# First pair's scores through ScalarE and GpSimd, loads of 112 rows instead of 128, half of the first f on ScalarE's queue

## The chip, the cores and the metric

The kernel runs on one core of a Trainium2 chip. The time is that of the device for one execution, in microseconds (us); the runs shown are three executions, given by their median. A profile is one more execution, recorded instruction by instruction; all its times count from the start of its span.

The engines, as the profile names them: PE (TensorE) multiplies matrices into PSUM, and PEld is its loading of weights; DVE (VectorE), ACT (ScalarE) and POOL (GpSimd) do elementwise work and scans; SP (SyncE) here only issues DMAs. SPq, DVEq and ACTq are the sequencers of those engines.

## The reference

```python
f = 1.0 / (1.0 + np.exp(-f_logit))                 # B, H, S, D = 4, 8, 768, 48
for t in range(S):
    state = f[:, :, t, :, None] * state + einsum('bhd,bhde', k[:, :, t], v[:, :, t])
    y[:, :, t] = einsum('bhd,bhde->bhe', q[:, :, t], state)
x = y as (3072 tokens, 384)
logits = x @ phi                                   # 32 slots, 4 for each of 8 experts
slot_input = softmax(logits over tokens).T @ x
slot_out[e] = relu(slot_input[e] @ w1[e]) @ w2[e]  # 384 -> 1024 -> 384
out = softmax(logits over slots) @ slot_out
```

It is a gated linear attention whose output goes through a mixture of experts with soft routing. All is float32.

## The kernel before

**Tiles.** The 32 heads are worked on as 16 pairs. In a tile of a pair the channels are rows: the first head has rows 0 to 47, the second rows 64 to 111 (`PW = 112`), and tokens are columns (768). The arrays in memory have 128 rows for each pair, so rows 48 to 63 and 112 to 127 are filler. A sequence is cut into 6 chunks of 128 tokens.

**One pair.** With the short names that the plan uses, and the lines of the profile:

- `lf`, `lk`, `lq`, `lv`: loads of f, k, q, v (L325, L754), issued by SP.
- `e` (ACT, L330) is exp(-f) with a running sum, `ln` (ACT, L334) is ln(1 + that), `L` (DVE, L338) its cumulative sum within each chunk, a scan.
- `g` and `p` (ACT, L341 and L344) are exp(L) and exp(-L). `dk` (L347) multiplies k by g, `dq` (L347) multiplies q by p; these run on POOL or DVE by pair.
- `pbx` and `pend` (POOL, L321 and L359) copy the decays at the ends of chunks, from p, for the state.
- `kt` (PE, L367) transposes k, `kte` (L321, tile kta) copies that out of PSUM.
- `sc` (PE, L379) are the scores k·q of each chunk for both heads, in two halves of three chunks each. `mask` (DVE, L384) multiplies them by a triangle of ones and zeros on the way from PSUM to the tile scb: two instructions for each pair.
- `kv` (PE, L413), then `scan` (DVE, L417) makes the states. `ia` (PE, L404) multiplies the masked scores by v, `ie` (PE, L427) adds q times state, `ye` (ACT, L321, tile yT) copies the result out of PSUM.
- `lg`, `xtr`, `xe` make the logits and the transposed y for the experts.

For pair 0 everything up to `dq` is done in two halves of 384 tokens, so that it starts on half a load.

**What sets the order.** Each operation is declared with an engine, an assumed duration and a due time; the class `Plan` runs a model of the engines over them, and the instructions are then written out in the order that the model found. Every engine works through its own instructions strictly in that order, whatever happens on the chip. For the first three pairs the table `START` sets due times by hand. SP's loads have due times too, with an assumed rate, and no more than eight loads are outstanding: the ninth waits until the first has landed, and so on. The score tile is double (scb), the PSUM is cut into three units of two banks (`a`) and two of one bank (`b`), which the plan hands out; `sc`, `kt`, `y` and `xt` share the three.

Two things at the start of the program touch the change: ACT's first instruction loads its table of functions (L229), and the first two loads of SP are the halves of pair 0's f (L754).

After the 16 pairs the experts follow (PE lines L502 to L712), whose weights w1 and w2 SP loads all along, into tiles that have come free.

Of the kernel before, what the change touches and what calls it, by code (L numbers as in the profile page):

```python
# [11 lines left out]
ALU = mybir.AluOpType  # L12
# [201 lines left out]
def gla_soft_moe_kernel(ctx: ExitStack, tc: tile.TileContext, q, k, f, v, vt, phi, w1, w2, out):  # L214
# [14 lines left out]
    nc.scalar.preload_act_table_set("natural_log_exp_and_others")  # L229
# [11 lines left out]
    fb = [P([128, S], f"fb{i}") for i in range(N_F)]  # L241
    Lb = [P([128, S], f"Lb{i}") for i in range(N_L)]
# [83 lines left out]


# [44 lines left out]
    def score(o, i, h):  # L372

        u = unit(("sc", i, h))
        for m in range(3):
            cs = slice(C * (3 * h + m), C * (3 * h + m) + C)
            for r in range(2):
                rs = slice(64 * r, 64 * r + D)
                nc.tensor.matmul(  # L379
                    u[:, 512 * r + C * m : 512 * r + C * m + C], kb[i % N_K][rs, cs], qb[i % N_Q][rs, cs], start=True, stop=True,  # L380
                )

# [344 lines left out]
    def warm(due, n, us=0.9):  # L727
# [11 lines left out]
        L=(-99, -98), dk=(-97, -95), dq=(-96, -94.5), mask=(-94.3, -92),  # L739
        kt=(-99, -96), sc=(-98, -95),  # L740
    )
    for n, (name, i) in enumerate(

        [("e", 1), ("ln", 1), ("kte", 0), ("e", 2), ("g", 1), ("p", 1), ("ln", 2), ("e", 3), ("ye", 0), ("kte", 1), ("g", 2), ("p", 2), ("ln", 3), ("ye", 1)]
# [3 lines left out]
        + [("pbx", 0), ("dk", 1), ("pend", 0)]  # L748
# [3 lines left out]

    def load_half(o, dst, src, cs):
        nc.sync.dma_start(dst[:, cs], src[:, cs])  # L754

    def attention(i):
# [12 lines left out]
        if i == 0:  # L769
            for h, cs in enumerate(HALVES):  # L770
                op("lf", {"SP": 0.45}, load_half, fb[0], f[0], cs, w=F_[h : h + 1], due=-99, kb=192)
        else:
            op("lf", {"SP": 0.45}, load, fb[i % N_F], f[i], w=F_, due=z - (25 if i > 1 else 18.5), kb=384)
        op("lk", {"SP": 0.45}, load, kb[i % N_K], k[i], w=K, due=z - 14, kb=384)
        if i == 0:

            for h, cs in enumerate(HALVES):
                op("lq", {"SP": 0.45}, load_half, qb[0], q[0], cs, w=Q[h : h + 1], due=-12 + 0.7 * h, kb=192)
        else:
            op("lq", {"SP": 0.45}, load, qb[i % N_Q], q[i], w=Q, due=z - 12, kb=384)  # L780
# [222 lines left out]
    for o in order:  # L1003
# [4 lines left out]
        new = list(nc.cur_bb.bb.instructions)[n0:]  # L1008
        if o.name in ("lw1", "lw2"):
# [20 lines left out]
    def general_pair(i):  # L1030
# [4 lines left out]
        nc.sync.dma_start(ft, f[i].unsqueeze(1).broadcast_to([128, NE4, S]))  # L1035
        nc.sync.dma_start(kq, k[i])
        nc.sync.dma_start(qt, q[i])
# [47 lines left out]
def _layout(inputs):  # L1085
# [52 lines left out]
```

## Time and profile before

| what | value |
|---|---|
| median of 3 runs | 168.49 us (167.91 to 168.71) |
| profiled execution, its own time | 168.29 us |
| its span, first to last instruction | 166.6 us |
| mean granted clock of TensorE | 0.984 |
| busy share of the span: PE, DVE, ACT, POOL | 92%, 70%, 57%, 54% |
| moved by DMA | 54.05 MB, mean 325 GB/s |
| the three loads of f, k and q of a pair | 384 KB each |

A row of the timeline reads: start, duration (both in us), engine, line, operation, written tile <- read tiles, shape, count; in brackets the idle time of the engine just before, and what ended it. Durations overlap a little: the next instruction of an engine starts up to 0.1 us before the recorded end of the one before. A busy PE is not PE at its peak. A row of the list of groups gives busy time in total and the mean of one instruction in ns. In the chain of waits each piece is followed back from the last instruction to what released it.

### The profile page before, as it was taken

Reading aid. Unit: us, or ns where it says so; the run is one execution under the profiler, and the core shown is the slowest. Engines: PE = TensorE matmul, PEld = TensorE weight load, DVE = VectorE, ACT = ScalarE, POOL = GpSimd, SP = SyncE. Lnnn points to the kernel's source line nnn. Section 1 sums busy time; section 2 is a strip of 40 time slices with the busy share of each in tenths; the row PEclk is TensorE's granted clock in tenths of the full one; section 3 lists DMA queues with packets and bytes.
Section 4 is the critical chain, followed back from the end, with each engine's and each line's share of the span. In section 5 each row is a group of like instructions: output and inputs, shape, how many; then the busy total and the mean of one; then the engine's idle time right before and its main releaser. Section 6 shows DMA issues by size and latency. Waiting matters only on the chain.

```text
span 166.6 us, 6386 instructions
## 1 busy us (share of the span) xinstructions
PE 153.7 (92%) x2724; PEld 123.3 (74%) x2724; DVE 116.6 (70%) x167; ACT 94.2 (57%) x166; POOL 89.9 (54%) x87
## 2 busy tenths in 40 slices
PE   5999999999999999999998999999899999999800
PEld 2367879889998969889896889988655449788700
DVE  4899999989979876898996989838432216043330
ACT  5899597967977949678783872631521121232310
POOL 5108969889889886897997889660000001000000
PEclk9999999999999999999999999999999999999985
DMA  5999999999999999999997559999999792055784
GB/s 134 320 407 370 390 399 398 399 398 393 395 393 397 397 397 399 396 398 398 398 377 248 182 173 293 340 363 407 398 398 389 233 360 85 6 215 211 281 295 151
DMA packets 20609, 54.05 MB, mean 325 GB/s; under 512 B 2288, under 2 KB 2912, under 8 KB 20576
## 3 DMA queue, kind: packets, MB, share of 16 engines
q1 hardware_dynamic: 20432, 53.34, 86.2%
q8 instruction: 22, 0.36, 0.9%
q10 hardware_dynamic: 144, 0.26, 0.4%
q14 instruction: 11, 0.09, 0.1%
HBM read 48.87 MB, written 4.72 MB: 322 GB/s over the span
## 4 chain that ended last, share of the span: by engine, by line
PE 67%; DVE 14%; POOL 5%; issue 4%; DMA 3%; ACT 3%; SPq 1%; POOLq 0%; ACTq 0%; DVEq 0%
PE sc L379 10%; PE y L404 9%; PE po L670 7%; PE up L625 7%; PE y L427 6%; PE kv L413 5%; PE kt L367 5%; DVE Lb L338 5%; PE xt L438 4%; PE pl L459 3%; PE pf L712 3%; DMA kb<-in_k_dram 3%; DVE scb L384 3%; POOL ce L545 2%; PE pi L502 2%
## 5 line engine op out<-in xcount | busy, mean ns | idle before, releaser
L347 POOL TENSOR_TENSOR kb<-kb,gb 112x768 f32<-112x768 f32 x15 | 27.4, 1830 | 16.3 <-ACT gb L341 12.8
L338 DVE TENSOR_TENSOR_SCAN Lb<-starts,fb 112x768 f32<-112x768 f32 (+1 forms) x17 | 35.1, 2063 | 1.6 <-ACT fb L334 1.6
L384 DVE TENSOR_TENSOR scb<-sc,mask 128x768 f32<-128x768 f32 x32 | 29.2, 950 | 4.0 <-PE sc L379 3.9
L321 POOL COPY pbx<-pb 112x240 f32<-112x240 f32 x16 | 26.6, 1663 | 4.6 <-ACT pb L344 4.6
L379 PE MATMUL sc<-qb,kb 48*128 48x128 f32 x384 | 26.5, 282 | 0.5 <-DVE kta L321 0.4
L404 PE MATMUL y<-scb,va 128*48 128x128 f32 (+1 forms) x384 | 25.9, 276 | 0.0
L379 PEld LDWEIGHTS sc<-qb,kb 48*128 48x128 f32 x384 | 22.9, 187 | 3.4 <-DVE kta L321 0.6
L321 ACT COPY yT<-y 112x768 f32<-112x768 f32 x16 | 12.8, 798 | 19.6 <-PE y L427 19.6
L347 POOL TENSOR_TENSOR qb<-qb,pb 112x768 f32<-112x768 f32 x13 | 23.7, 1827 | 0.0
L404 PEld LDWEIGHTS y<-scb,va 128*48 128x48 f32 (+1 forms) x384 | 21.9, 130 | 0.8 <-DVE scb L384 0.4
L545 POOL TENSOR_TENSOR ce<-ce,cm 128x256 f32<-128x256 f32 x4 | 4.6, 1156 | 29.7 <-DVE cm L542 29.3
L321 DVE COPY kta<-kt 128x672 f32<-128x672 f32 x14 | 11.8, 846 | 7.6 <-PE kt L367 7.6
L341 ACT ACTIVATE gb<-Lb 112x768 f32<-112x768 f32 (+1 forms) x17 | 13.7, 805 | 4.9 <-DVE Lb L338 4.9
L334 ACT ACTIVATE fb<-fb,one 112x768 f32<-112x768 f32 (+1 forms) x17 | 15.2, 897 | 0.6
L330 ACT ACTIVATE fb<-fb 112x768 f32<-112x768 f32 (+1 forms) x17 | 13.7, 805 | 2.7 <-DMA fb<-in_f_dram 2.7
L427 PE MATMUL y<-qb,sb 48*48 48x128 f32 x320 | 14.6, 285 | 0.0
L413 PE MATMUL kv<-va,kta 128*64 128x48 f32 (+1 forms) x384 | 14.4, 220 | 0.0
L413 PEld LDWEIGHTS kv<-va,kta 128*64 128x64 f32 (+1 forms) x384 | 12.4, 130 | 2.6 <-ACT kta L321 0.8
L344 ACT ACTIVATE pb<-Lb 112x768 f32<-112x768 f32 (+1 forms) x17 | 13.5, 792 | 0.0
L427 PEld LDWEIGHTS y<-qb,sb 48*48 48x48 f32 x320 | 11.1, 162 | 2.7 <-DVE sb L417 2.4
L367 PE MATMUL kt<-ident,kb 112*128 112x112 f32 x96 | 12.7, 266 | 0.2 <-POOL kb L347 0.2
L321 DVE COPY w1a<-pf 128x512 f32<-128x512 f32 x9 | 5.8, 687 | 9.5 <-ACT w1a L321 9.5
(154 smaller groups left out, 276.9 us busy)
## 6 DMA issues: line engine op xcount, KB each, us to landing
w1a<-in_w_dram SPq DMA_DIRECT2D x34, 384.0 KB, 7.6
kb<-in_k_dram SPq DMA_DIRECT2D x16, 384.0 KB, 7.4
fb<-in_f_dram SPq DMA_DIRECT2D x15, 384.0 KB, 7.3
qb<-in_q_dram SPq DMA_DIRECT2D x15, 384.0 KB, 7.3
va<-in_v_dram SPq DMA_DIRECT2D x16, 288.0 KB, 7.3
out_dram<-w1a SPq DMA_DIRECT2D x6, 512.0 KB, 3.5
scb<-in_w_dram SPq DMA_DIRECT2D x4, 384.0 KB, 6.9
out_dram<-w1a SPq DMA_DIRECT2D x5, 256.0 KB, 3.9
```

The costliest lines, as they stand in the source:

```text
L321: {"ACT": nc.scalar.copy, "DVE": nc.vector.tensor_copy, "POOL": nc.gpsimd.tensor_copy}[o.eng](dst, src)
L330: nc.scalar.activation(t, t, AF.Exp, scale=-1.0, accum_out=esum[:, n : n + 1])
L334: nc.scalar.activation(t, t, AF.Ln, bias=one[:PW])
L338: nc.vector.tensor_tensor_scan(Lb[i % N_L][:PW, cs], flat(starts)[:PW, cs], fb[i % N_F][:PW, cs], 0.0, op0=ALU.mult, op1=ALU.add)
L341: nc.scalar.activation(gb[i % N_G][:PW, cs], Lb[i % N_L][:PW, cs], AF.Exp)
L347: (nc.vector if o.eng == "DVE" else nc.gpsimd).tensor_tensor(t, t, by, op=ALU.mult)
L367: nc.tensor.transpose(u[:, C * m : C * m + PW], kb[i % N_K][:PW, C * m : C * m + C], ident[:PW, :PW])
L379: nc.tensor.matmul(u[:, 512 * r + C * m : 512 * r + C * m + C], kb[i % N_K][rs, cs], qb[i % N_Q][rs, cs], start=True, stop=True,)
L384: nc.vector.tensor_tensor(scb[i % N_SC][:, :, h], un["sc", i, h].rearrange("p (r x) -> p r x", r=2)[:, :, : 3 * C].rearrange("p r (m t) -> ...
L404: nc.tensor.matmul(u[rows(at), y_cols(m)], va[:, v0 : v0 + (D if at else 64)], scb[i % N_SC][:, r, h, m % 3], start=m % 3 == 0, stop=False ...
L413: nc.tensor.matmul(u[rows(r), :, m], ktb[i % N_KT][:, m, rows(r)], vb[i % N_V][:, m, r], start=True, stop=True)
L427: nc.tensor.matmul(u[at : at + D, y_cols(m)], sb[i % N_S][rs, :, m - 1], qb[i % N_Q][rs, C * m : C * m + C], start=False, stop=m in (2, 5) ...
```

## The change

Four edits, all about the start of the program, except that the second holds for all pairs.

1. Half 0 of pair 0's scores is no longer multiplied by the triangle on DVE. ACT copies it from PSUM (`smc`), and POOL then clears the upper triangle in place with one affine select over 128 x 768 (`sms`). Half 1 and all other pairs keep `mask`.
2. The arrays f, q and k have 112 rows for each pair in memory and are loaded as 112 rows: 336 KB instead of 384. The rows left out are never read.
3. The second half of pair 0's f is loaded by a DMA that ACT issues as its first instruction, ahead of its table load; SP issues only the first half.
4. `START` changes: `smc` stands ahead of pair 0's `kte`, `g` and `p` of pair 1 ahead of `e` of pair 2, and `e` of pair 3 behind `kte` of pair 1. A wait is added too: POOL's `pbx` of pair 0 now waits until the second `dq` of pair 0 is done on DVE.

```diff
-    nc.scalar.preload_act_table_set("natural_log_exp_and_others")
...
     fb = [P([128, S], f"fb{i}") for i in range(N_F)]
+    nc.scalar.dma_start(fb[0][:PW, S // 2 :], f[0][:, S // 2 :])
+    nc.scalar.preload_act_table_set("natural_log_exp_and_others")
...
+    def load_rows(o, dst, src, cs=slice(0, S)):
+        nc.sync.dma_start(dst[:PW, cs], src[:, cs])
...
+    def score_copy(o, i, h):
+        copy(o, scb[i % N_SC][:, :, h], un["sc", i, h].rearrange("p (r x) -> p r x", r=2)[:, :, : 3 * C].rearrange("p r (m t) -> p r m t", t=C))
+
+    def score_select(o, i, h):
+        t = scb[i % N_SC][:, :, h]
+        nc.gpsimd.affine_select(t, t, pattern=[[0, 2], [0, 3], [1, C]], compare_op=ALU.is_ge, fill=0.0, base=0, channel_multiplier=-1)
...
-        [("e", 1), ("ln", 1), ("kte", 0), ("e", 2), ("g", 1), ("p", 1), ("ln", 2), ("e", 3), ("ye", 0), ("kte", 1), ("g", 2), ("p", 2), ("ln", 3), ("ye", 1)]
+        [("e", 1), ("ln", 1), ("smc", 0), ("kte", 0), ("g", 1), ("p", 1), ("e", 2), ("ln", 2), ("ye", 0), ("kte", 1), ("e", 3), ("g", 2), ("p", 2), ("ln", 3), ("ye", 1)]
...
-        + [("pbx", 0), ("dk", 1), ("pend", 0)]
+        + [("pbx", 0), ("sms", 0), ("dk", 1), ("pend", 0)]
...
-            for h, cs in enumerate(HALVES):
-                op("lf", {"SP": 0.45}, load_half, fb[0], f[0], cs, w=F_[h : h + 1], due=-99, kb=192)
+            op("lf", {"SP": 0.45}, load_rows, fb[0], f[0], HALVES[0], w=F_[:1], due=-99, kb=168)
...
-            op("mask", {"DVE": 0.95}, score_mask, i, h, r=[key], w=[SC[h]], due=START["mask"][h] if i == 0 else z - T + 6.1 + h, free=[key])
+            if (i, h) == (0, 0):
+                op("smc", {"ACT": 0.82}, score_copy, i, h, r=[key], w=[SC[h]], due=START["smc", 0], free=[key])
+                op("sms", {"POOL": 1.3}, score_select, i, h, r=[SC[h]], w=[SC[h]], due=START["sms", 0])
+            else:
+                op("mask", {"DVE": 0.95}, score_mask, i, h, r=[key], w=[SC[h]], due=START["mask"] if i == 0 else z - T + 6.1 + h, free=[key])
...
+        if o.name == "dq" and o.args[0] == 0:
+            first_q = new[-1].name
+        if o.name == "pbx" and o.args == (0,):
+            tc.add_manual_dep(new[-1], first_q, ...Sync..., reason="behind the products")
...
-        a[n] = y.reshape(NP, 128, S)
+        a[n] = y.reshape(NP, 128, S)[:, :PW]
```

PE's instructions keep their order. The three places where order moves, first ACT from pair 1's `e` on. The names in these rows are tiles: fb is f, gb and pb are exp(L) and exp(-L), kta the copied transposes, scb the scores, yT the result; the number behind a name is its buffer. Before:

```order
L330 ACTIVATE fb_68,esum<-fb_68 112x768
L334 ACTIVATE fb_68<-fb_68,one 112x768
L321 COPY kta<-kt 128x672
L330 ACTIVATE fb_69,esum<-fb_69 112x768
L341 ACTIVATE gb_75<-Lb_71 112x768
L344 ACTIVATE pb_77<-Lb_71 112x768
L334 ACTIVATE fb_69<-fb_69,one 112x768
L330 ACTIVATE fb_67,esum<-fb_67 112x768
L321 COPY yT_92<-y 112x768
L321 COPY kta<-kt 128x672
L341 ACTIVATE gb_74<-Lb_70 112x768
```

With the change, up to the same instruction, the g of pair 2:

```order
L336 ACTIVATE fb_67,esum<-fb_67 112x768
L340 ACTIVATE fb_67<-fb_67,one 112x768
L323 COPY scb_86<-sc 128x2x384
L323 COPY kta<-kt 128x672
L347 ACTIVATE gb_76<-Lb_72 112x768
L350 ACTIVATE pb_78<-Lb_72 112x768
L336 ACTIVATE fb_68,esum<-fb_68 112x768
L340 ACTIVATE fb_68<-fb_68,one 112x768
L323 COPY yT_93<-y 112x768
L323 COPY kta<-kt 128x672
L336 ACTIVATE fb_66,esum<-fb_66 112x768
L347 ACTIVATE gb_75<-Lb_71 112x768
```

The score copy is new between pair 1's `ln` and pair 0's `kte`; pair 3's `e` moved from ahead of `ye` to directly ahead of pair 2's `g`.

POOL at the same time, before, from pair 0's `pbx` on:

```order
L321 COPY pbx_88<-pb_76 112x48x5
L347 TENSOR_TENSOR kb_79<-kb_79,gb_75 112x768
L359 COPY pends<-pb_76 112x6
L321 COPY pbx_89<-pb_77 112x48x5
L359 COPY pends<-pb_77 112x6
```

and with the change:

```order
L323 COPY pbx_89<-pb_77 112x48x5
L394 AFFINE_SELECT scb_86<-scb_86 128x2x384
L353 TENSOR_TENSOR kb_80<-kb_80,gb_76 112x768
L365 COPY pends<-pb_77 112x6
L323 COPY pbx_90<-pb_78 112x48x5
```

The affine select stands between pair 0's `pbx` and pair 1's `dk`.

DVE, before, from the last `dq` of pair 0 on:

```order
L347 TENSOR_TENSOR qb_81<-qb_81,pb_76 112x384
L384 TENSOR_TENSOR scb_85<-sc,mask 128x2x384
L338 SCALAR_TENSOR_TENSOR Lb_71<-starts,fb_68 112x768
L384 TENSOR_TENSOR scb_85<-sc,mask 128x2x384
L417 SCALAR_TENSOR_TENSOR sb_90<-kv,pbx_88 112x288
```

and with the change:

```order
L353 TENSOR_TENSOR qb_82<-qb_82,pb_77 112x384
L344 SCALAR_TENSOR_TENSOR Lb_72<-starts,fb_67 112x768
L397 TENSOR_TENSOR scb_86<-sc,mask 128x2x384
L430 SCALAR_TENSOR_TENSOR sb_91<-kv,pbx_89 112x288
```

One `mask` is gone, so that pair 1's scan `L` (shown as SCALAR_TENSOR_TENSOR, written to Lb) directly follows pair 0's last `dq`. SP loses its second load, and from pair 3's f on some loads change places with neighbours.

More of the change, by code (lines that the diff above doesn't have):

```diff
@@ L1008, in gla_soft_moe_kernel @@
         new = list(nc.cur_bb.bb.instructions)[n0:]
+        if o.name == "dq" and o.args[0] == 0:
+            first_q = new[-1].name
+        if o.name == "pbx" and o.args == (0,):
+            tc.add_manual_dep(
+                new[-1], first_q, mybir.DependencyInfo(mybir.DependencyClass.Sync, mybir.DependencyReason.DATA), reason="behind the products",
+            )
         if o.name in ("lw1", "lw2"):
```

18 lines of the change are left out of this document (8 added, 10 removed).

## The prediction, made before the change was run

> **What bounds the kernel now.** I read the chain of waits first, in order of time.
>
> ```profile
> 22.91 0.76 DVE kta L321
> 23.71 0.94 PE sc L379 x12
> ...
> 25.42 1.39 PE y L404 x23
> ...
> 53.37 0.47 PE pl L459 x8
> ```
>
> From 23.71 to 53.8 every piece is PE, and what leaves PE later starts from a PE instruction again. PE keeps its order, so the forecast is a forecast of one moment: when the second half of pair 2's scores starts (23.71). It waits for kta, pair 2's transposes, which DVE copies behind a scan. The timeline shows what stands ahead of it.
>
> ```profile
> 3.24 0.52 ACT L330 ACTIVATE fb<-fb 112x384 f32<-112x384 f32 x1 [1.17 <-DMA fb<-in_f_dram]
> 7.17 0.51 ACT L344 ACTIVATE pb<-Lb 112x384 f32<-112x384 f32 x1
> 8.26 0.84 ACT L330 ACTIVATE fb<-fb 112x768 f32<-112x768 f32 x1 [0.57 <-DMA fb<-in_f_dram]
> 9.22 0.94 ACT L334 ACTIVATE fb<-fb,one 112x768 f32<-112x768 f32 x1
> 10.07 0.70 ACT L321 COPY kta<-kt 128x672 f32<-128x672 f32 x1
> 10.66 0.84 ACT L330 ACTIVATE fb<-fb 112x768 f32<-112x768 f32 x1
> 14.29 0.83 ACT L330 ACTIVATE fb<-fb 112x768 f32<-112x768 f32 x1
> 15.12 0.78 ACT L321 COPY yT<-y 112x768 f32<-112x768 f32 x1
> 15.80 0.72 ACT L321 COPY kta<-kt 128x672 f32<-128x672 f32 x1
> 17.26 0.84 ACT L341 ACTIVATE gb<-Lb 112x768 f32<-112x768 f32 x1 [0.74 <-DVE Lb L338]
> ```
>
> The last row is pair 2's g (g2). POOL's dk2 follows it, then DVE's dq2, the scan L3, kta, and PE at 23.71. ACT stood idle 0.74 us ahead of g2 for DVE's scan L2.
>
> ```profile
> 7.88 0.95 DVE L347 TENSOR_TENSOR kb<-kb,gb 112x384 f32<-112x384 f32 x1
> 8.85 0.56 DVE L347 TENSOR_TENSOR qb<-qb,pb 112x384 f32<-112x384 f32 x1
> 9.32 0.95 DVE L384 TENSOR_TENSOR scb<-sc,mask 128x768 f32<-128x768 f32 x1
> 10.19 1.76 DVE L338 TENSOR_TENSOR_SCAN Lb<-starts,fb 112x768 f32<-112x768 f32 x1
> 13.60 1.96 DVE L347 TENSOR_TENSOR qb<-qb,pb 112x768 f32<-112x768 f32 x1
> 15.48 1.75 DVE L338 TENSOR_TENSOR_SCAN Lb<-starts,fb 112x768 f32<-112x768 f32 x1
> 7.75 0.67 POOL L321 COPY pbx<-pb 112x240 f32<-112x240 f32 x1 [4.64 <-ACT pb L344]
> 12.91 1.83 POOL L347 TENSOR_TENSOR kb<-kb,gb 112x768 f32<-112x768 f32 x1 [4.50 <-ACT gb L341]
> 15.55 2.08 POOL L321 COPY pbx<-pb 112x240 f32<-112x240 f32 x1
> 18.18 1.83 POOL L347 TENSOR_TENSOR kb<-kb,gb 112x768 f32<-112x768 f32 x1 [0.41 <-ACT gb L341]
> ```
>
> These rows also show that POOL and DVE keep each other out. pbx takes 0.67 alone, but 2.08 when it starts beside the scan of 15.48: the scan's remaining 1.68 plus 0.40. dq1 (13.60) ends 0.82 after dk1 (12.91 + 1.83 = 14.74). Of pair 0's two half products on k, the one beside pbx took 0.95; its like on q, with POOL idle, took 0.56.
>
> **The change part by part.** Fewer bytes (edits 2 and 3). ACT's e of pair 1 waited 0.57 us for its load. Up to its end SP's queue held 2 x 192 of f, 384 of k, 192 of q and its own 384, 1344 KB; with the change seven eighths of that, 1176.
>
> ```profile
> 2.00:3.00 1.00, 0.96 (x1) 0.50 (x2) 0.96 (x6) 0.07 (x1) 0.83 (x11) 1.00 0.96 272
> 5.00:6.00 1.00, 1.00 (x2) 0.43 (x2) 0.81 (x2) 0.97 (x3) 0.00 (x0) 1.00 0.89 333
> 6.00:7.00 1.00, 1.00 (x2) 0.00 (x0) 0.86 (x2) 0.80 (x3) 0.00 (x0) 1.00 0.89 298
> 7.00:8.00 1.00, 1.00 (x4) 0.33 (x3) 1.00 (x3) 0.68 (x2) 0.26 (x1) 1.00 0.91 325
> ```
>
> In these one-microsecond windows the last column is GB/s. At their 319 (mean of the last three) the 168 KB less are 0.53 us: the load lands at 8.26 - 0.53 = 7.73. ACT is free for it at about 7.60 (7.17 + 0.51, less the usual overlap), so e1 starts at 7.73, a gain of 0.53. In the chain from 23.71 on stands no load, so the rest of the 12.5% is worth 0. In SP's queue pair 3's f falls behind pair 2's k and pair 1's v; its e moves back too, from 14.29 to past 16, which covers the 624 KB (1.96 us at 319 GB/s).
>
> The first f load, half the size, may land earlier or later than 3.24. It carries 24 KB less (at 272 GB/s: -0.09 us). But its second half now comes from another queue at the same time; in the worst case that half's 168 KB go first, 144 KB more than before: 144/272 = +0.53. By 3.00 that one window had moved 272 KB, 80 more than the first half, so much of the second went ahead of the landing before too; I sit between, at +0.15. The table load (1.28 us, ended 2.07) moves behind ACT's issue. SP's issue of a load took 0.43 there; with it the table is ready at 2.5, covered by the 1.17 of waiting. But the only DMA that ACT issues now was recorded much longer:
>
> ```profile
> 1.80 0.43 SPq L325 DMA_DIRECT2D kb<-in_k_dram  x1
> 159.08 1.61 ACTq L719 DMA_DIRECT2D out_dram<-w1a  x1
> 0.79 1.28 ACT L229 ACT_TABLE_LOAD   x1 [0.79 <-PEq L1125]
> ```
>
> At 1.61 the table would end at 0.79 + 1.61 + 1.28 = 3.68 and the first e would come 0.44 late. So the bounds of the start are -0.09 and +0.53, and +0.15 stands. As e1 waits for its own load until 7.73 in any case, only what exceeds 0.13 counts: +0.02.
>
> Mask off DVE (edit 1), pbx behind the products (edit 4). pbx no longer meets the second dk: 0.95 becomes 0.56, and DVE is through pair 0's products at 8.85 + 0.56 - 0.39 = 9.02. The mask's 0.95 are gone too. The scan L1 then waits for ln1 alone: 7.73 + 0.96 (8.26 to 9.22) + 0.94 = 9.63. L1 runs 9.65 to 11.41 instead of 10.19 to 11.95. Of 1.34 us taken from DVE, 0.54 arrive: ACT is next.
>
> What replaces the mask. ACT's copy smc starts at 7.73 + 0.96 + 0.85 (9.22 to 10.07) = 9.54; PE's scores are long there. The yT copies, also out of two banks of PSUM, take 0.80, so smc ends at 10.34. POOL's select, sms, could then start, but DVE is in L1 until 11.41, and I let POOL wait for it as pbx did. The length of sms is not in the trace. In the list of groups (mean in ns last) and the timeline near 88 us are its nearest rows:
>
> ```profile
> L292 POOL TENSOR_SCALAR_AFFINE_SELECT mask<-mask 128x128 f32<-128x128 f32 x1 | 0.3, 294 | 0.1
> L290 POOL MEMSET mask<- 128x128 f32 x1 | 0.2, 205 | 0.0
> L308 POOL MEMSET emask<- 128x256 f32 x1 | 0.4, 360 | 0.0
> ```
>
> ```profile
> 87.72 1.24 POOL L522 TENSOR_SCALAR pin<-pin,nmb 128x384 f32<-128x384 f32 x1
> 88.24 1.75 DVE L338 TENSOR_TENSOR_SCAN Lb<-starts,fb 112x768 f32<-112x768 f32 x1
> ```
>
> The memsets (128 and 256 columns) give 0.155 for 128 columns and 0.05 fixed. Lower bound: the select at a memset's rate, 0.05 + 6 x 0.155 = 0.98. Upper bound: the in-place TENSOR_SCALAR, 1.24 for 384 columns, doubled: 2.48. I take the select's own row with that fixed part, 0.05 + 6 x 0.244 = 1.5, as it is the same operation. sms ends at 11.41 + 1.5 = 12.91.
>
> Behind it on POOL stands dk1, which waited for g1 anyway: g1 at 11.43, done 12.28, so dk1 runs from 12.91, as before. dq1, L2 and pair 1's masks stay where they were. PE, though, waits for sms with pair 0's ia: from 12.97, for 1.45 (1.39 for 23 of 24, from the chain), then ie, and yT follows 0.96 after ie's start (as at 20.75 after 19.79):
>
> ```profile
> 19.79 0.91 PE L427 MATMUL y<-qb,sb 48*48 48x128 f32 x20
> 20.75 0.80 ACT L321 COPY yT<-y 112x768 f32<-112x768 f32 x1 [1.09 <-PE y L427]
> ```
>
> That puts yT at 12.97 + 1.45 + 0.96 = 15.38, against 15.12. By the new order of ACT now come yT, kte1, e3, g2: 0.68 (15.12 to 15.80), 0.60 (10.07 to 10.66), 0.83 (14.29 to 15.12), and g2 starts at 17.49. Before, e3 was done ahead of yT and g2 waited in an idle 0.74. That idle time is used up, and g2 comes 0.23 late: dk2, dq2, L3, kta and PE at 23.71 with it. The sum is +0.23 + 0.02 = **+0.25 us**: the earlier load and the shorter DVE queue are eaten by the select's wait and by e3.
>
> On the profiled execution's own 168.29 that is 168.54. It lies 0.20 under the median of the runs, inside their spread of 0.80, so I forecast 168.5 for the median, hardly told from no change. A measurement of this kernel can tell about 0.5% (0.84 us) from none: faster means below 167.65, slower above 169.33.
>
> **The rivals.** (a) The select need not wait for the scan. For it: pin, like the select with a single input, is at work from 87.72 for 1.24, and the scan that starts beside it at 88.24 takes its undisturbed 1.75. Against it: pbx, a plain copy, did wait. Then sms ends at 10.40 + 1.5 = 11.90, ia starts at 11.95, and yT waits only for ACT: g1 at 11.43, then p1, e2, ln2 and yT behind it by 0.75, 0.75, 0.96 and 0.85 (a row's length less the usual overlap; ln behind e as at 9.22) = 14.74, and g2 at 14.74 + 2.11 = 16.85, a gain of 0.41: 167.88, at best (e1 at 7.60) 167.75. It crosses 167.65 only with luck elsewhere.
>
> (b) Slower: the select takes pin's price. Each 0.1 us of sms beyond 1.5 passes one for one through ia, yT, kte1, e3 and g2 to PE. At 2.48: +0.25 + 0.98 = 169.52. It decides from a length of 1.5 + (169.33 - 168.54) = 2.29 on. For it: 3.2 ns a column in pin's row; against it: 2.3 in the select's own, fixed part and all.
>
> (c) Loads of 112 rows take as long as those of 128. Nothing in the trace excludes it: the queue moved 128-row loads nearly throughout. Then e1 stays at 8.26, everything from L1 on is 0.53 later than in my sum: 168.54 + 0.53 = 169.07, and with the start's +0.53 not absorbed, 169.5. The Trainium skill speaks for it (SBUF — State Buffer, "Door 1: The DMA port swizzle"): a transfer's rate depends on the ports its partitions reach, and by its table dropping partitions 112 to 127 only halves the rows behind four ports of sixteen, while the other twelve carry all eight rows. By that rule a load bound by ports would gain nothing; no run here shows it yet.
>
> **How the numbers follow.** My own sum 0.56, with a range of 168.0 to 168.9 (select 0.98 to 1.5, or the start at +0.53, 0.40 of it unabsorbed); (a) 0.20; (b) 0.12; (c) 0.07; 0.05 for what no row shows. Faster: 0.3 of (a), the low tail of the rest: 0.11. Slower: most of (b), nearly half of (c), 0.05 elsewhere: 0.18. Same: 0.71. The range of 8 in 10 goes from (a) at its best, 167.7, to just under the point where (b) decides, 169.3.
>
> **What would show it.** In the changed profile: e1 at about 7.7 with little idle time (else (c)); the second dk of pair 0 at 0.56; L1 at 9.65; sms reaching past 12.7 though smc ended near 10.3 (else (a)), and its length less the scan's remainder; ia directly behind it; g2 at 17.5 with no idle time ahead, and PE's second half of sc at about 23.9. The forecast is wrong if g2 comes below 16.9 or above 18.3, or if PE's chain after pair 2 has lost or won time of its own.

## The result: 17% slower, and DMA becomes the bound

The changed kernel takes 198.57 us (median of 4 runs, 196.38 to 202.0), where the kernel before takes 168.6 beside it (4 runs, 167.91 to 169.04): a ratio of 1.168 with a 95% interval of 1.164 to 1.172. Two of the four runs (200.44 and 202.0) were in a slower state, so that the ratio is that of the other two, 196.38 and 196.71. Forecast was 168.5. The profiled execution took 196.71 us, 28.42 more than the one before (168.29); its span is 195.0.

The page of the changed kernel: the chain of waits by engine, the rate of DMA in 40 slices of the span, and two rows of the list of issues, whose last column is the median time in us from issue to landing.

```profile
DMA 49%; PE 40%; POOL 2%; ACT 2%; issue 1%; DVE 1%; SPq 0%; ACTq 0%; POOLq 0%; DVEq 0%
...
GB/s 165 279 272 287 298 309 282 270 281 287 284 264 298 241 272 284 266 260 285 270 262 238 238 211 217 90 293 318 394 399 397 395 245 379 84 5 269 268 295 153
...
w1a<-in_w_dram SPq DMA_DIRECT2D x34, 384.0 KB, 10.5
kb<-in_k_dram SPq DMA_DIRECT2D x16, 336.0 KB, 10.3
```

Half of the chain is now DMA. Until late in the span nothing goes above 310 GB/s, though the load of k is smaller than before; the load of w1, which was not edited, takes 10.5 us to land too (7.6 before). The list of waits, first of the kernel before, then of the changed one (us in total, times, longest):

```profile
ACT fb L330 <- DMA fb<-in_f_dram: 2.7, 4, 1.2
```

```profile
ACT fb L336 <- DMA fb<-in_f_dram: 43.3, 12, 6.0
```

ACT now waits for f 12 times, 43.3 us in total instead of 2.7. Three windows of 40 us show why; the last two columns are the busy share of the DMA engines and GB/s, the one ahead of them the granted clock of TensorE. Before:

```profile
0.00:40.00 40.00, 37.19 (x548) 28.51 (x550) 36.10 (x40) 31.33 (x51) 27.18 (x39) 1.00 0.97 360
40.00:80.00 40.00, 39.78 (x720) 35.06 (x715) 34.85 (x42) 30.60 (x55) 34.53 (x26) 1.00 1.03 396
80.00:120.00 40.00, 38.81 (x684) 33.23 (x680) 31.08 (x48) 22.23 (x39) 27.54 (x23) 1.00 0.89 314
```

And after:

```profile
0.00:40.00 40.00, 30.59 (x399) 23.47 (x401) 26.45 (x33) 25.66 (x43) 23.06 (x37) 0.92 0.99 270
40.00:80.00 40.00, 33.33 (x548) 29.15 (x544) 27.04 (x29) 22.44 (x38) 20.98 (x19) 0.91 1.04 276
80.00:120.00 40.00, 33.35 (x505) 29.64 (x506) 23.34 (x31) 20.80 (x38) 20.64 (x18) 0.87 0.98 248
```

The busy share reads the same, 1.03 and 1.04, at 396 and at 276 GB/s: the engines are as busy, and move 30% less. One thing stands in the rows of before that the prediction did not use: DMA was full already, so that its loads had no room to become slower. PE, at 39.78 of 40 us, was waiting for nothing, as the prediction had it. In the changed kernel PE idles, and its granted clock reads 0.87 to 0.92; with loads of 128 rows, below, it reads 1.00 again. What lowers the clock no run separates: in `e12`, below, PE was busy for only 32.48 of the first 40 us and the clock read 1.00.

The head of the program, up to the moment that the prediction forecast, from the timeline of the changed kernel:

```profile
4.22 0.52 ACT L336 ACTIVATE fb<-fb 112x384 f32<-112x384 f32 x1 [1.60 <-DMA fb<-in_f_dram]
8.53 0.55 DVE L353 TENSOR_TENSOR kb<-kb,gb 112x384 f32<-112x384 f32 x1
8.57 0.83 ACT L336 ACTIVATE fb<-fb 112x768 f32<-112x768 f32 x1
10.50 1.76 DVE L344 TENSOR_TENSOR_SCAN Lb<-starts,fb 112x768 f32<-112x768 f32 x1 [0.95 <-ACT fb L340]
11.22 1.70 POOL L394 TENSOR_SCALAR_AFFINE_SELECT scb<-scb 128x768 f32<-128x768 f32 x1 [1.00 <-ACT scb L323]
12.97 1.53 PE L417 MATMUL y<-scb,va 128*48 128x128 f32 x24 [0.17 <-POOL scb L394]
14.43 0.91 PE L440 MATMUL y<-qb,sb 48*48 48x128 f32 x20
14.72 0.94 ACT L340 ACTIVATE fb<-fb,one 112x768 f32<-112x768 f32 x1
15.57 0.78 ACT L323 COPY yT<-y 112x768 f32<-112x768 f32 x1
16.97 0.84 ACT L336 ACTIVATE fb<-fb 112x768 f32<-112x768 f32 x1
17.81 0.83 ACT L347 ACTIVATE gb<-Lb 112x768 f32<-112x768 f32 x1
24.25 0.94 PE L385 MATMUL sc<-qb,kb 48*128 48x128 f32 x12 [0.61 <-DVE kta L323]
24.78 0.85 ACT L336 ACTIVATE fb<-fb 112x768 f32<-112x768 f32 x1 [2.93 <-DMA fb<-in_f_dram]
```

PE's second half of pair 2's scores starts at 24.25, 0.54 later than before. That is all that was lost by then. Half a microsecond later, at 24.78, comes the first of ACT's long waits for f, 2.93 us; the other 28 us are lost behind it.

### The profile page after: what moved, and what is told of

It is laid out like the page before. It is cut to its first block, busy times and chain, and to the rows that moved or that the text cites. A ratio compares the mean times of both kernels' runs of the same rounds, so it can differ in the third digit from the quotient of the medians.

```text
span 195.0 us, 6379 instructions
## 1 busy us (share of the span) xinstructions
PE 163.2 (84%) x2724; PEld 133.2 (68%) x2724; DVE 113.2 (58%) x166; ACT 94.0 (48%) x167; POOL 82.9 (43%) x88
## 4 chain that ended last, share of the span: by engine, by line
DMA 49%; PE 40%; POOL 2%; ACT 2%; issue 1%; DVE 1%; SPq 0%; ACTq 0%; POOLq 0%; DVEq 0%
DMA qb<-in_q_dram 16%; DMA fb<-in_f_dram 13%; DMA va<-in_v_dram 10%; PE po L683 6%; PE up L638 6%; DMA w1a<-in_w_dram 5%; DMA kb<-in_k_dram 5%; PE sc L385 5%; PE y L417 5%; PE pf L725 3%; PE kv L426 3%; PE y L440 3%; PE pi L515 2%; PE xt L451 2%; PE kt L373 2%; PE pl L472 1%
## 5 line engine op out<-in xcount | busy, mean ns | idle before, releaser
L385 PE MATMUL sc<-qb,kb 48*128 48x128 f32 x384 | 30.4, 311 | 16.4 <-ACT yT L323 15.2
L353 POOL TENSOR_TENSOR kb<-kb,gb 112x768 f32<-112x768 f32 x15 | 28.2, 1879 | 33.3 <-ACT gb L347 17.8
L385 PEld LDWEIGHTS sc<-qb,kb 48*128 48x128 f32 x384 | 26.7, 213 | 19.3 <-issue 16.3
L336 ACT ACTIVATE fb<-fb 112x768 f32<-112x768 f32 (+1 forms) x17 | 13.7, 804 | 43.3 <-DMA fb<-in_f_dram 43.3
L344 DVE TENSOR_TENSOR_SCAN Lb<-starts,fb 112x768 f32<-112x768 f32 (+1 forms) x17 | 30.6, 1801 | 3.5 <-ACT fb L340 3.5
L417 PE MATMUL y<-scb,va 128*48 128x128 f32 (+1 forms) x384 | 28.8, 295 | 0.2 <-POOL scb L394 0.2
L417 PEld LDWEIGHTS y<-scb,va 128*48 128x48 f32 (+1 forms) x384 | 25.4, 144 | 0.7 <-POOL scb L394 0.3
L323 POOL COPY pbx<-pb 112x240 f32<-112x240 f32 x16 | 16.2, 1010 | 6.5 <-DVE qb L353 6.5
L426 PE MATMUL kv<-va,kta 128*64 128x48 f32 (+1 forms) x384 | 18.0, 249 | 0.0
L426 PEld LDWEIGHTS kv<-va,kta 128*64 128x64 f32 (+1 forms) x384 | 15.8, 157 | 3.1 <-ACT kta L323 0.8
L340 ACT ACTIVATE fb<-fb,one 112x768 f32<-112x768 f32 (+1 forms) x17 | 15.3, 897 | 0.6
L430 DVE TENSOR_TENSOR_SCAN sb<-kv,pbx 112x288 f32<-112x288 f32 x16 | 12.0, 751 | 3.1 <-PE kv L426 3.1
L350 ACT ACTIVATE pb<-Lb 112x768 f32<-112x768 f32 (+1 forms) x17 | 13.5, 795 | 0.0
L440 PEld LDWEIGHTS y<-qb,sb 48*48 48x48 f32 x320 | 11.1, 162 | 2.7 <-DVE sb L430 1.4
## 6 DMA issues: line engine op xcount, KB each, us to landing
w1a<-in_w_dram SPq DMA_DIRECT2D x34, 384.0 KB, 10.5
fb<-in_f_dram SPq DMA_DIRECT2D x15, 336.0 KB, 10.5
qb<-in_q_dram SPq DMA_DIRECT2D x15, 336.0 KB, 10.5
```

What stands on the lines that cost most here:

```text
L323: {"ACT": nc.scalar.copy, "DVE": nc.vector.tensor_copy, "POOL": nc.gpsimd.tensor_copy}[o.eng](dst, src)
L336: nc.scalar.activation(t, t, AF.Exp, scale=-1.0, accum_out=esum[:, n : n + 1])
L340: nc.scalar.activation(t, t, AF.Ln, bias=one[:PW])
L344: nc.vector.tensor_tensor_scan(Lb[i % N_L][:PW, cs], flat(starts)[:PW, cs], fb[i % N_F][:PW, cs], 0.0, op0=ALU.mult, op1=ALU.add)
L353: (nc.vector if o.eng == "DVE" else nc.gpsimd).tensor_tensor(t, t, by, op=ALU.mult)
L385: nc.tensor.matmul(u[:, 512 * r + C * m : 512 * r + C * m + C], kb[i % N_K][rs, cs], qb[i % N_Q][rs, cs], start=True, stop=True,)
```

## The experiments

Two theories stood at first; their letters stand in the expectations. **The loads** (R): loading 112 rows instead of 128 lowers the rate of DMA, by the number of rows (R1) or by the layout of the arrays in memory (R2). **The queue** (Q): ACT's DMA in a second queue, or the changed order of SP's loads, disturbs it.

### Is it the loads?

`e1_edits134_128rows` is the changed kernel with arrays and loads of 128 rows again; everything else of it, the order of SP's loads too, stays.

```diff
-    nc.scalar.dma_start(fb[0][:PW, S // 2 :], f[0][:, S // 2 :])
+    nc.scalar.dma_start(fb[0][:, S // 2 :], f[0][:, S // 2 :])
...
-        nc.sync.dma_start(dst[:PW, cs], src[:, cs])
+        nc.sync.dma_start(dst[:, cs], src[:, cs])
...
-        a[n] = y.reshape(NP, 128, S)[:, :PW]
+        a[n] = y.reshape(NP, 128, S)
```

> The changed kernel with edit 2 undone: f, q and k stand with 128 rows in memory and are loaded as 128 rows again (384 KB), all other edits and the order of all instructions kept. Theory R (a load of 112 rows is slow by itself): DMA is back at about 398 GB/s in the full slices and the time is within 1 us of before, 168.3 to 169.6; by the order of ACT, which the changed profile bore out at the start, pair 2's second half of scores comes 0.2 to 0.6 us late, so 168.6 to 169.2. Theory Q (ACT's DMA in a second queue, or the changed order of SP's loads, disturbs the queue): the time stays above 190. For the moved mask alone: if POOL's select waits for the scan, g of pair 2 starts at 17.5 or later; if not, before 17.0.

Measured: 170.36 us, ratio 1.0116 (1.0082 to 1.0151). All but some 2 us of the loss is gone, so theory Q falls; the time lies 0.8 us above the range of R. Of its windows and its waits:

```profile
40.00:80.00 40.00, 39.42 (x712) 34.42 (x710) 35.27 (x42) 30.45 (x53) 33.51 (x25) 1.00 1.04 396
```

```profile
ACT fb L336 <- DMA fb<-in_f_dram: 11.1, 11, 1.9
```

The rate is back at 396 GB/s. What is left, 2 us and 11.1 us of waiting for f, is taken up below.

`e2_before_112packed` is the kernel before with edit 2 alone; `e3_before_112of128` loads 112 rows too, but out of the arrays of 128 rows, which tells the number of rows from the layout.

```diff
+    def load_rows(o, dst, src, cs=slice(0, S)):
+        nc.sync.dma_start(dst[:PW, cs], src[:, cs])        # e3: src[:PW, cs]
...
-            op("lf", {"SP": 0.45}, load, fb[i % N_F], f[i], ...)
+            op("lf", {"SP": 0.45}, load_rows, fb[i % N_F], f[i], ...)
```

> The kernel before with edit 2 alone: arrays of 112 rows for each pair, loads of 112 rows by SP, everything else and the order of SP's loads as before. Theory R: about 195 us, DMA near 275 GB/s in the first hundred us. Theory Q: 167 to 169 us, DMA near 398 GB/s.

> As the run before it, but the arrays keep 128 rows for each pair in memory and only 112 of them are loaded. Theory R1 (the number of rows of the load is what costs): the same as with packed arrays, about 195 us. Theory R2 (the packed arrays put the reads badly in memory; 344064 bytes for a pair instead of 393216): 166 to 169 us, since fewer bytes move at the old rate.

Measured, a single execution each: 207.62 and 207.21 us, 12 us more than R had. Edit 2 alone costs the whole loss and more, and the layout in memory makes no difference that can be seen. The waits for f, e2 and then e3:

```profile
ACT fb L333 <- DMA fb<-in_f_dram: 52.2, 15, 7.3
```

```profile
ACT fb L333 <- DMA fb<-in_f_dram: 53.4, 15, 7.1
```

Why edit 2 alone is slower than all four edits together (207 against 196.4 to 202.0) was a new question; `e12` answers it below.

### What does a load cost by its rows?

`e4_loads_alone` computes nothing (its output is zeros): it issues loads in the same way, 16 of each kind in a row.

```diff
+    def rows_112_packed(n):
+        nc.sync.dma_start(bufs[n % 8][:112], packed[n % NP])
...
+    for fn, r in ((full_128, 128), (rows_112_of_128, 112), (rows_112_packed, 112), ..., (rows_96, 96), (rows_80, 80), (rows_64, 64), (rows_120, 120), ...):
+        for n in range(16):
+            fn(n)
```

> A kernel of loads alone, no computation (its output is zeros): eleven stages of 16 loads each on SP's queue into eight tiles of 768 columns, each stage ended by eight small DVE copies: 128 rows; 112 rows out of 128; 112 rows packed; 128 rows of w1 (rows 12288 bytes apart in memory); 112 rows of w1; 96, 80, 64, 120 rows; 112 rows as 64 + 48; 128 again. From the changed profile: 1008 KB of 112-row loads and some 960 KB of 128-row loads for each pair at 275 GB/s together, the latter at 398, leave 212 GB/s for the former. Theory R1: all stages of 112 rows near 212 GB/s, 128 rows near 398. Theory R2: only the packed stage is slow. By the number of rows for each of 16 engines (112 is 7, 96 is 6, 80 is 5, 64 is 4): if every number other than 8 is slow, 96 and 80 are too; if odd numbers are what is slow, 112 and 80 are and 96 is not.

Windows out of the middle of the stretches, in this order: 128 rows; 112 of 128; 112 packed; 96; 80; 64; 120; and 112 rows as two loads of 64 and 48. Last column GB/s.

```profile
14.00:21.00 7.00, 1.07 (x7) 0.00 (x0) 1.00 1.04 399
26.00:33.00 7.00, 0.00 (x0) 0.00 (x0) 1.00 1.03 268
46.00:53.00 7.00, 0.00 (x0) 0.00 (x0) 1.00 1.04 269
...
105.00:111.00 6.00, 0.00 (x0) 0.00 (x0) 1.00 1.04 251
124.00:128.00 4.00, 0.00 (x0) 0.00 (x0) 1.00 1.04 250
140.00:150.00 10.00, 0.73 (x5) 0.00 (x0) 1.00 1.04 195
160.00:170.00 10.00, 0.46 (x3) 0.00 (x0) 1.00 0.97 243
...
180.00:190.00 10.00, 0.00 (x0) 0.00 (x0) 1.00 0.96 238
```

A row is 3072 bytes, so 128 rows (393 kB) at 399 GB/s take 0.99 us and 112 rows (344 kB) at 268 take 1.28: an eighth fewer bytes, 30% more time. (The estimate in the expectation, 212 GB/s, was too low.) In the same way 120 rows take 1.52, 96 take 1.17, 80 take 0.98 and 64 take 1.01. Cutting the 112 rows into loads of 64 and 48 rows is no way out: the two together take 1.45. w1's rows, 12,288 bytes apart in memory, gave the same: 400 GB/s for 128 of them, 266 for 112. The Trainium skill (SBUF — State Buffer, "Door 1: The DMA port swizzle") says that the rate follows from the ports that the partitions reach; its table puts eight rows behind the fullest port for 64, 80, 96, 112, 120 and 128 rows alike. The rows agree for 64, 80 and 128; for 96, 112 and 120 the load is 0.2 to 0.5 us slower than that rule would have it, and the measurement decides.

Rows four times as long (12,288 bytes, in `e8_loads_and_selects_alone`, whose expectation and other half come below) tell a cost for each packet from one for each byte: first 128 rows, then 112.

```profile
42.00:62.00 20.00, 0.77 (x5) 0.00 (x0) 1.00 1.01 428
78.00:112.00 34.00, 0.92 (x6) 0.00 (x0) 1.00 1.00 243
```

That is 3.67 us for 1573 kB and 5.66 for 1376 kB. The extra time grows from 0.3 to 2.0 us as the rows grow fourfold, so it grows with the bytes and is no fixed cost of a packet or of a load. Both theories of the expectation miss the factor: it neither stays at 1.3 nor falls, it rises to 1.54. In the same run 112 rows in partitions 16 to 127 landed 1.19 us apart, a little faster than those in 0 to 111, and 48 rows 1.0 us apart, as long as 64. The stretch of 112 rows of 1536 bytes waited for DVE, and those of 32 and 16 rows were paced by SP's issuing (0.46 us each); they are not read.

But 48 loads of f, k and q at 0.30 us more each make 14.4 us, not 28.4; and the loads of w1 and v have 128 rows still. `e11_loads_mixed` sets loads of 112 and 128 rows beside each other, again without any work (output zeros).

```diff
+    for form, r in (
+        ([(rows, 128)] * 2, 128), ([(rows, 112), (w, 128)], 112), ([(rows, 112), (w, 128), (w, 128), (w, 128)], 112),
+        ([(rows, 112)] * 3 + [(v, 128), (w, 128), (w, 128)], 112), ([(rows, 128)] * 3 + [(v, 128), (w, 128), (w, 128)], 128),
+        ([(rows, 112)] * 3 + [(w, 112)] * 3, 112),
+    ):
+        for n in range(24):
+            fn, k = form[n % len(form)]
+            fn(n, k)
```

> Loads alone again, without any of the work (the output is zeros, so the time is that of the loads only). Six stretches of 24 loads each, all issued by SP: (1) 128 rows; (2) 112 and 128 rows in turn; (3) one of 112 rows, then three of 128; (4) as the changed kernel has them for one pair: three of 112 rows, one of v (128 rows of 2304 bytes), two of w1 (128 rows); (5) the same with 128 rows in place of 112; (6) all of 112. In the changed kernel the DMA moves 270 GB/s from 0 to 40 us and 276 from 40 to 80, though between loads of 112 rows stand nearly as many of 128. Theory M (each load takes its own time, 0.98 or 1.28 us, whoever stands beside it): stretch 2 moves 737 kB in 2.26 us, 326 GB/s; 3, 1524 kB in 4.22 us, 361; 4, 2113 kB in 3 x 1.28 + 0.74 + 2 x 0.98 = 6.54 us, 323; 5 about 400; 6 267. Theory N (a load of 112 rows slows the loads of 128 beside it too, as several are under way at once): 2 and 4 near the kernel's 270, 3 between 270 and 330; 5 and 6 as in M. By M the changed kernel's loads would need some 20% less time than they took, and something else than the number of rows holds its DMA at 270; by N the rows are enough.

```profile
10.00:20.00 10.00, 0.00 (x0) 0.00 (x0) 1.00 1.03 407
32.00:60.00 28.00, 0.77 (x5) 0.00 (x0) 1.00 1.04 263
66.00:84.00 18.00, 0.00 (x0) 0.00 (x0) 1.00 1.04 311
96.00:112.00 16.00, 0.00 (x0) 0.00 (x0) 1.00 1.04 296
125.00:137.00 12.00, 0.00 (x0) 0.00 (x0) 1.00 1.04 400
147.00:165.00 18.00, 0.00 (x0) 0.00 (x0) 1.00 1.04 279
```

The six rows are the six stretches. Theory M falls, N holds: 112 and 128 rows in turn move 263 GB/s, not 326, less even than 112 rows alone. A pair of them (737 kB) takes 2.80 us, where their own times add up to 2.26; by the copies that DVE makes as the loads land, the full loads come some 1.7 us behind the load ahead of them, those of 112 rows 1.1. One load of 112 rows in four pulls the queue down to 311. The loads of one pair of heads (stretch 4, 2113 kB) take 7.14 us, those with 128 rows (stretch 5, 2261 kB) 5.65: for 16 pairs 23.8 us more. At the 273 GB/s that the kernel's own windows show up to 80 us it would be 7.74, or 33 us more. The 28.4 lost lie between the two. What the loads meet at inside the chip no run shows. If the rows are dealt out evenly, 112 rows are seven for each of the 16 DMA engines and 128 are eight; that engines with seven get in each other's way, where engines with eight do not, is only argued.

### What the order of the loads is worth

`e5_edits134_replanned` has edits 1, 3 and 4 on loads of 128 rows, as `e1`, but the plan again counts these loads as 384 KB (`kb=384`), so that SP's loads are planned as they were before. `e12_all_edits_order_384` does the same to the changed kernel itself, with loads of 112 rows; the lines are those of `e12`. In both pairs only the order of SP's loads differs.

```diff
-            op("lf", {"SP": 0.45}, load_rows, fb[i % N_F], f[i], w=F_, ..., kb=336)
+            op("lf", {"SP": 0.45}, load_rows, fb[i % N_F], f[i], w=F_, ..., kb=384)
```

> Edits 1, 3 and 4 with loads of 128 rows, as in the first of these runs, which took 170.4; but there the order and pace of SP's loads was planned for 336 KB, here for 384. In that run PE was 0.69 late at pair 2, 0.87 at 63 us, 2.15 at 93 us, and ACT waited 11.1 us for loads of f in eleven places. Theory P (those later losses come from the order of loads planned for smaller ones): ACT's waits for f shrink to a few us and the time is 168.8 to 169.3. If the losses come from the start itself, they stay and the time is 170 or more.

> The changed kernel with all four edits, loads of 112 rows, but the plan counts each load of f, k and q as 384 KB, as it did before the change, so that SP issues its loads in the order and at the pace of before. Edit 2 alone took 207.62 and 207.21 us with loads planned for 384 KB, the changed kernel 196.7 in its profiled run with loads planned for 336 KB. Theory O (the order in which loads of 112 and of 128 rows stand in the queue makes the difference): 205 to 208, with the DMA at 240 to 262 GB/s up to 120 us, as in the two runs of edit 2 alone, instead of 270 and 276. Rival (one of the edits 1, 3 and 4 makes the loss smaller): 196 to 199, the DMA at 270 to 276 up to 80 us.

Measured: `e5` 168.14 us, ratio 1.0007 (0.9987 to 1.0026); `e12` 205.72 (a single execution). The 2 us that `e1` still lost were the order of its loads, planned for less than it loaded: ACT's waits for f (11.1 us there) shrink to 1.7, below the 2.7 of before, and the three other edits together cost nothing that can be measured (theory P had expected 168.8 to 169.3). With 112 rows the order works the other way: planned for 336 KB 196.4 to 202.0, planned for 384 KB 205.7, near `e2` and `e3`, as theory O said; 4 to 9 us, which one execution can't tell more closely. Its rate agrees only in part: 269 GB/s in the first 40 us, where O had 262 at most, then 260 and 247. In `e12` the long loads stand differently among those of w1 and v; `e11` shows that this matters, but which order is the best was not tried.

The waits of `e5`, and the first 40 us of `e12`:

```profile
ACT fb L331 <- DMA fb<-in_f_dram: 1.7, 2, 1.5
```

```profile
0.00:40.00 40.00, 32.48 (x460) 24.63 (x460) 31.88 (x35) 27.52 (x46) 25.48 (x38) 1.00 1.00 269
```

### The start of the program

`e7_edit3` is the kernel before with edit 3 alone (the second half of the first f from ACT's queue, 128 rows); `e6_edits14` has edits 1 and 4 alone, `e10_edits14_again` is the same kernel once more.

```diff
-    nc.scalar.preload_act_table_set("natural_log_exp_and_others")
...
+    nc.scalar.dma_start(fb[0][:, S // 2 :], f[0][:, S // 2 :])
+    nc.scalar.preload_act_table_set("natural_log_exp_and_others")
...
-                op("lf", {"SP": 0.45}, load_half, fb[0], f[0], cs, w=F_[h : h + 1], due=-99, kb=192)
+                op("lf", {"SP": 0.45}, (lambda o, *a: None) if h else load_half, fb[0], f[0], cs, w=F_[h : h + 1], due=-99, kb=192)
```

(The plan still has SP's second load, which then issues nothing, so that all other loads keep their order.)

> The kernel before with edit 3 alone: ACT issues the second half of the first f, ahead of its table load; SP's other loads, their order and all else as before. Theory S: the first e starts at about 4.0, all of the start comes 0.7 to 0.8 us later, and the time is 0.5 to 0.9 us longer, about 168.9. If the late landing was due to SP's k and q coming earlier in the queue, not to the second queue, it is as late here, since they come earlier here too.

> The kernel before with edits 1 and 4 alone (score half through ACT and POOL, the new order on ACT, pbx behind the products); loads of 128 rows, both halves of the first f issued by SP; the plan was run anew for it, so that some of SP's later loads change places. In the run of edits 1, 3 and 4 the first f landed 0.81 us later (4.05 against 3.24) and PE's second half of pair 2's scores came 0.69 late (24.40 against 23.71). Theory S (the late start is the second queue's, edit 3): here the first e of ACT starts at 3.24 again, and edits 1 and 4 by themselves move PE's moment by -0.1 to +0.3; 168.0 to 168.6 if no load comes late afterwards. Theory M (the moved mask costs by itself): +0.5 or more at that moment, 168.8 or above.

> Edits 1 and 4 alone once more, as the profile of the first run of them had the second half of the first q landing late, beside more rounds. Expected: e0 at 3.24 +- 0.1 as before, sms for 1.70 beside the scan L1 or about 0.86 alone, e3 directly ahead of g2 with g2 at 17.2 to 17.5, and the time within 0.2% of before (0.998 to 1.002).

Measured: `e7` 168.42 us, ratio 1.0004 (0.9987 to 1.0021); `e6` 168.16, 0.9988 (0.9965 to 1.0011); `e10` 167.89, 0.9990 (0.9972 to 1.0008). None can be told from no change; the 0.5 to 0.9 us that theory S gave `e7` did not come. In the profiled execution of `e6` the second half of the first q landed late, so its timeline is not read; that of `e10` is. The first e, of `e7` and then of `e10`:

```profile
4.08 0.52 ACT L331 ACTIVATE fb<-fb 112x384 f32<-112x384 f32 x1 [1.49 <-DMA fb<-in_f_dram]
```

```profile
3.25 0.52 ACT L330 ACTIVATE fb<-fb 112x384 f32<-112x384 f32 x1 [1.17 <-DMA fb<-in_f_dram]
...
23.51 0.94 PE sc L379 x12
```

The late start is edit 3's: 4.08 against 3.24 with loads of 128 rows, 0.84 of the 0.98 us in the changed kernel. In windows of 1 us its DMA moves 12, 224 and 415 kB from 1.00 to 4.00, so by 4.08 (0.08 us more at 363) some 680 kB have gone, three and a half halves of 197 kB; before, some 344 kB had gone at 3.24. So some 480 kB of the other half of f and of the loads behind it went through ahead of the first half's landing, instead of some 150. Whether the second queue does that or the loads of k and q, which SP issues 0.46 us earlier here too, no run separates. In `e7` the second half of pair 2's scores starts at 24.12, 0.41 late; in `e10` (last row, out of the chain of waits) at 23.51, 0.20 early, but there the load of pair 1's f landed some 0.3 us earlier than before and e1 started at 7.93 instead of 8.26, so that the stretch behind it is 0.13 longer; with edits 1, 3 and 4 together (`e5`) at 24.03, 0.32 late, and the end moved by less: the span of `e5` is 166.4, that of before 166.6. A shift of a few tenths at this moment can no longer be found at the end.

The other half of `e8` runs four selects of 128 x 768 without a wait between them, then four beside scans on DVE.

```diff
+    for _ in range(4):
+        select(alone[:, :, 0])
...
+    for x in range(4):
+        nc.vector.tensor_tensor_scan(scan[:112], one[:112], zero[:112], 0.0, ...)
+    for _ in range(4):
+        select(beside[:, :, 0])
```

> No computation of the reference (its output is zeros). On POOL four affine selects of 128 x 768 with DVE idle, then four more beside four of DVE's scans of 112 x 768. If the select excludes the scan as pbx did: 1.0 to 1.5 alone, and beside the scans both are longer by each other's length. If it does not: 1.70 both times, as recorded in the changed kernel, and the scans stay at 1.76. On SP's queue eight stages of loads: 128 and 112 rows of 1536 bytes; 128 and 112 rows of 12288 bytes; 112 rows into partitions 16 to 127; 48, 32 and 16 rows of 3072 bytes. The stages alone so far gave for one load 0.98 us for 128, 80 and 64 rows, 1.18 for 96 and 1.28 for 112. Ports theory (what counts is how many rows lie behind the fullest of 16 ports of the tile's memory, and how the engines meet there): 112 rows are slower than 128 by the same factor of about 1.3 at any length of row, 32 rows take half the time of 64, 48 rows as long as 64, since they lie behind the same eight ports, 16 rows behind four ports as long as 32. Packet theory (a cost of each packet): the factor falls with the length of the row, and time goes with the number of rows.

The instructions of the select's line (duration in ns: shortest, median, longest; the times of the first and the last start in us), and from the timeline a scan that did not have to wait for a select, and one of those among the last four selects:

```profile
L30 POOL TENSOR_SCALAR_AFFINE_SELECT alone<-alone x4: 865/1532/3149, 10.7 to 17.1; 128x768 f32<-128x768 f32 x4
L30 POOL TENSOR_SCALAR_AFFINE_SELECT beside<-beside x4: 865/2200/2201, 17.9 to 23.4; 128x768 f32<-128x768 f32 x4
```

```profile
13.74 1.69 DVE L36 TENSOR_TENSOR_SCAN scan<-one,zero 112x768 f32<-112x768 f32 x1
...
20.42 2.23 DVE L39 TENSOR_TENSOR_SCAN scan<-one,zero 112x768 f32<-112x768 f32 x1
```

A select by itself takes 0.87 us. Beside scans three of the four take 2.20 (the first began ahead of the scan and took 0.87), and the scans 2.23 instead of 1.69. So they do hold each other up, and rival (a), that the select need not wait for the scan, falls. (The first four were not all alone: DVE had two scans and a memset at the time, which is why only the shortest is used.) The Trainium skill (SBUF — State Buffer, "SBUF: two separate sides") says that VectorE with two inputs in SBUF and GpSimd hold a shared pair of ports one after the other, each for its whole instruction. These rows agree that they wait for each other, as pbx did in the kernel before, but not that the wait is the whole instruction: a scan becomes 0.54 us longer beside a select of 0.87.

`e9_edits14_e3_early` was an attempt at a faster kernel than both: edits 1 and 4 with pair 3's e ahead of the first yT again.

```diff
-        [..., ("e", 2), ("ln", 2), ("ye", 0), ("kte", 1), ("e", 3), ("g", 2), ...]
+        [..., ("e", 2), ("ln", 2), ("e", 3), ("ye", 0), ("kte", 1), ("g", 2), ...]
```

> Edits 1 and 4 alone (arrays of 128 rows, both halves of the first f from SP), and in edit 4 the e of pair 3 goes back ahead of the first yT, where it stood before the change. By my sum the select delays yT by about 0.3 us and e3 directly ahead of g2 then costs what is left of ACT's idle 0.74 us. With e3 early, yT should start at 15.3 to 15.5 and g2 at yT + 0.68 + 0.60, 16.6 to 16.8 unless it still waits for the scan L2; before it started at 17.26. So PE's second half of pair 2's scores should come 0.1 to 0.4 us ahead of the 23.71 of before, and the time 168.0 to 168.5 where before has 168.3 to 168.6: ratio 0.997 to 1.000. The rival, that the start of the program does not set the end at all, gives 1.000 whatever happens at 23.7.

Measured: 168.5 us, ratio 1.0024 (1.0007 to 1.0041). A miss. (Its profiled execution took 169.36, well above its median, so only the head of it is read.)

```profile
15.18 0.83 ACT L330 ACTIVATE fb<-fb 112x768 f32<-112x768 f32 x1
...
16.01 0.78 ACT L321 COPY yT<-y 112x768 f32<-112x768 f32 x1
...
17.30 0.85 ACT L341 ACTIVATE gb<-Lb 112x768 f32<-112x768 f32 x1
```

yT comes at 16.01 instead of the 15.3 to 15.5 expected, as it now waits for e3, and g2 at 17.30 instead of 16.6 to 16.8. With the copy of the scores added, ACT has no idle time left between pair 1's g and pair 2's g, so moving e3 among them leaves g2 where it was. No version tried here is faster than the kernel before by more than its interval.

## Why the prediction was wrong, point by point

**The step that failed** is the price of the bytes. The prediction took the rate of the queue as given: "At their 319 the 168 KB less are 0.53 us", and "In the chain from 23.71 on stands no load, so the rest of the 12.5% is worth 0". The bytes fell by an eighth, and the rate by a third: 1.28 us instead of 0.98 for a load of f, k or q, and slower loads of w1 and v beside them. The whole loss comes from this; without it the same edits measure 1.0007. It shows ahead of 23.71 already: by the forecast's own terms pair 3's f should have landed at about 14.9 (13.5 before, less 0.53, plus 1.96); it landed at about 17.0 (issued at 7.89, 9.1 us to landing), just as ACT came to its e at 16.97.

**The bound ahead of it** was one-sided. Rival (c) went as far as loads of 112 rows taking as long as those of 128, priced at 169.07, with a chance of 0.07. That a smaller load might take longer was not among the cases, though the trace of before had no load of 112 rows to bound it by. And from "no load stands in the chain" it does not follow that the loads have room. They had none to lose: DMA was busy for 0.97 and 1.03 of its time up to 80 us. With the queue full, a load that becomes slower has nothing to hide behind; the 0.71 for no change left that case out.

**The first f.** +0.15, between -0.09 and +0.53, was mis-sized: +0.98 in the changed kernel, +0.84 with 128 rows. The upper bound let only the second half of f go first, 168 KB; by the bytes counted above, loads that stand behind it in SP's queue went ahead of the landing too. The other half of that step was right: ACT's issue took 0.44 us, not 1.61, and the table load did not delay e. e1 then followed at 8.57 with no wait. Its load had landed at about 7.8 (issued at 2.28, 5.5 us to landing), close to the 7.73 forecast, but by luck: with edit 2 alone (`e2`) the same load landed at about 9.1 (2.75 + 6.3), where before it took until 8.2.

**The mask off DVE, pbx behind the products.** Right: the second dk took 0.55 (0.56 forecast). L1 started 0.85 after its forecast, which is the late first e.

**The select.** That it waits for the scan was right, and shown by itself in `e8`; that it ends at 12.91 was right to 0.01 by two errors that cancel. The scan ended 0.85 late (12.26 for 11.41), and the select's own length was about 0.7 to 0.9, not 1.5. The two rows used to bound it from below, the memsets, lay above it. Rival (b), 2.48, is far off.

**From yT to PE.** Half right. ia came behind the select (12.97, as forecast), and e3 stood directly ahead of g2 with no idle time there. But yT did not wait for PE, as the sum has it (ie at 14.43 + 0.96 gives 15.39): it followed ln2 on ACT without idle time, at 15.57. Rival (a) works out that path, 14.74 for a scan that ends at 11.41; with the 0.85 by which the scan ended late it gives 15.59. So the late first f decided yT, and the select did not. g2 came at 17.81 for 17.49, PE's second half of the scores at 24.25 for "about 23.9": +0.54 where the sum had +0.25. That the moment was met so nearly is luck too: e1 came 0.84 late, and the stretch from e1 to it was 0.55 shorter than forecast (15.68 for 16.23).

**What the forecast rested on** was that one moment in PE's chain sets the end. The prediction named the condition (wrong "if PE's chain after pair 2 has lost or won time of its own"), and it is just this that happened, from 24.78 on. Nor does the moment set the end to tenths of a microsecond where the loads are as before: 0.32 late in `e5` and 0.41 in `e7` left 1.0007 and 1.0004.

## What to carry to other kernels

Fewer bytes is not less time: price a changed load by its own measured duration, above all if its number of rows changes, and don't keep the old rate. Before costing a slower or differently shaped transfer at nothing, read the DMA share and the GB/s of each stretch together: here a share of 1.03 at 396 GB/s, with no load in the chain, meant loads that were just in time, and a share of 1.04 at 276 a queue held up by its loads of 112 rows. One shape of load can slow the others in its queue, so measure it in the mixture in which it will run.

## What the runs showed of the hardware that was not expected

- Loads of 112 rows of 3072 bytes moved 268 GB/s, of 120 rows 243, of 96 rows 251, where 128 rows moved 399; 80 rows took the same time as 128 (0.98 and 0.99 us), and 112 rows cut into 64 and 48 took 1.45. (At 120 rows the DMA share is lower too, 0.97 against 1.03 to 1.04, so it may not be the same cause.) With rows of 12,288 bytes it was 243 against 428.
- Loads of 128 rows are slowed by loads of 112 rows beside them: 263 GB/s in turn, 311 with one in four.
- With the first load split over SP's and ACT's queues, the e behind its first half started 0.84 us later than with two halves issued by SP one after the other (4.08 against 3.24).
- An in-place affine select of 128 x 768 took 0.87 us, 1.1 ns a column, where the one of 128 x 128 took 294 ns.
- The same loads in another order cost 4 to 9 us with 112 rows (196.4 to 202.0, and a single 205.7) and 2 us with 128 rows (168.1 and 170.4), in opposite directions.
